# Two interleaved layers of linear attention and a squared-ReLU network: reordering the first stage and moving ten stores of the k/q weights

## The chip, the core and the metric

The kernel runs on one core of a Trainium2 chip. A core has a matrix engine (TensorE, PE in the profile, with its weight loads as PEld), a vector engine (VectorE, DVE), a scalar engine (ScalarE, ACT), a general engine (GpSimd, POOL) and a queue engine that here issues nearly all DMAs (SyncE, SP). Each engine runs its own list of instructions, and semaphores between them hold an instruction back until what it needs is there. The metric is the device time of one launch in microseconds; the median of three runs before the change is 1320.23 us.

## The reference

Two identical layers, each an attention block A and a network B, both on a residual stream `x` of 2048 rows by 640 columns:

```python
def _A_ref(x, wqkv, wo):                       # 32 heads of 20 columns
    qkv = (x @ wqkv).reshape(B, S, 3, H, Dh).transpose(2, 0, 3, 1, 4)
    q, k, v = qkv[0], qkv[1], qkv[2]
    phi = lambda t: jnp.where(t > 0, t + 1, jnp.exp(t)) + 1e-6
    pq, pk = phi(q), phi(k)
    kv = jnp.einsum("bhsd,bhse->bhde", pk, v)
    z = jnp.einsum("bhsd->bhd", pk)
    num = jnp.einsum("bhqd,bhde->bhqe", pq, kv)
    den = jnp.einsum("bhqd,bhd->bhq", pq, z)[..., None] + 1e-6
    return (num / den).transpose(0, 2, 1, 3).reshape(B, S, D) @ wo
def _B_ref(x, w1, b1, w2, b2):
    h = jnp.einsum("bsd,df->bsf", x, w1) + b1
    r = jnp.where(h > 0, h, 0)
    return jnp.einsum("bsf,fd->bsd", r * r, w2) + b2
x = A_x
x = x + _A_ref(_layernorm(x), A_wqkv, A_wo)
x = x + _B_ref(_layernorm(x), B_w1, B_b1, B_w2, B_b2)
x = x + _A_ref(_layernorm(x), A_wqkv, A_wo)
x = x + _B_ref(_layernorm(x), B_w1, B_b1, B_w2, B_b2)
```

## The kernel before

Every large product is made of three matmuls: each operand is split into a high part (a rounded copy) and a low part (what the rounding lost), and high times low, low times high and high times high are added in PSUM (`mm3`, L485). So each tile that goes into a product needs two parts: ScalarE writes the high one, VectorE then subtracts it to get the low one.

The rows are worked in 16 tiles of 128. A layer has three stages: phase A (the loop over t at L823), a transition (L960 to L1169) and the network (L1171 on). Phase A runs once through the 16 tiles, in layer 0 between about 7 and 194 us of the profile. In tile t:

- TensorE makes k and q of the tile with `part` (L574), in up to three pieces. The first goes to PSUM bank `xb[0]`, the second to `xb[1]`, the third to `xb[2]`. A tile listed in `LATE` (L43; in layer 0 tiles 9 and 11 to 15, in layer 1 tiles 8, 9, 11 and 13 to 15) makes only k in phase A, in two pieces of 320 columns; these are the q-less tiles of the title of the change, and their q is made in the transition by `late_q` (L968). The other tiles make k and q in pieces of 512, 512 and 256 columns.
- TensorE adds xᵀ·phi(k) of the tile before, t−1, to five accumulators: the strips `g_part` (L614), handed out by `gs` (L883). Every second tile it also makes two products for the last columns, `gt_part` (L620), each into a bank that a piece of k has left.
- ScalarE and VectorE turn a piece into phi: `Phi.exp` (L589, ScalarE, L591 in the profile) reads the piece in PSUM, `Phi.rest` (L594, VectorE, L598 and L599) reads it again. After the L599 of a piece its bank is free.
- For phi(k) ScalarE writes the high part (`k_post`, L783) and VectorE the low part (L793); both are the right operands of the strips, one tile later. The normalized rows are split in the same way (high L898, low L928).
- For tile t+1 the transposed rows `xT` are made ready. In layer 0 VectorE transposes in blocks (L461), ScalarE moves the blocks in 16 small copies (`move`, L803, with `turn_move`, L475), then ScalarE writes the high part (`xT_split`, L502) and VectorE the low part (L505). Eight of the 16 copies for tile t+1 are issued at the end of tile t−1 (`move(t + 2, AHEAD)`, L959), the other eight in tile t (`move(t + 1)`, L895). In layer 1 a pair of DMAs does this instead of the 16 copies.
- In tiles 1 to 13 of layer 0 the weights of the network are split on the side: `prep_step` (L809) puts up to four high parts (L301) and low parts (L313) into a tile.

The order of each engine's list is the order in which the code calls the engines; there is no scheduler, so a line that stands later in a tile waits behind all that stand before it on its engine. When a q-less tile has an even number, the list of banks is rotated at its end (L957): the first piece of tile 13 goes to the bank that the second piece of tile 12 had, and likewise for tiles 15 and 14.

The split k/q weights (`kq`, five tiles) are written to DRAM in layer 0 so that layer 1 can read them back: `keep_kq` (L195), ten DMAs of 640 KB on SP's queue, two each in tiles 11 to 15 (L832).

Of the kernel before, what the change touches and what calls it, by code (L numbers as in the profile page):

```python
# [16 lines left out]
NT = S // P  # L17
DC = D // P
# [47 lines left out]
def kernel(  # L66
# [25 lines left out]
    def bank(i, n=1):  # L92
        return PS[:, 512 * i : 512 * (i + n)]
# [17 lines left out]
    def ftile(name):  # L111
        return tmp.tile([P, D], F32, tag="f", name=name, bufs=F_BUFS)
# [38 lines left out]
    class FirstLoads:  # L151
# [19 lines left out]
        def low(self, n):  # L171
            for _ in range(min(n, len(self.halves))):
                u, raw = self.halves.pop(0)
                nc.vector.tensor_tensor(
                    out=u[:, 1], in0=raw, in1=u[:, 0].bitcast(F32), op=ALU.subtract
                )
# [18 lines left out]
    def keep_kq(c, j):  # L195
        nc.sync.dma_start(kept["kq", c][:, j], kq[c][:, j].bitcast(F32))
# [247 lines left out]
    def blocks_T(src):  # L444
        y = ftile("y")
        nc.vector.transpose(out=y, in_=src)  # L446
        return [y]
# [19 lines left out]
    def turn_move(yz, js):  # L467

        if len(yz) == 1:
            yz.append(ftile("z"))  # L470
        yv = yz[0].rearrange("p (j c q) -> p j c q", c=DC, q=B32)
        zv = yz[1].rearrange("p (c i q) -> p c i q", c=DC, q=B32)
        for j in js:
            for i in range(P // B32):
                nc.scalar.activation(  # L475
                    zv[j * B32 : (j + 1) * B32, :, i, :], yv[i * B32 : (i + 1) * B32, j], AF.Copy
                )
# [33 lines left out]
    def proj(ps, aT, w, cs=range(DC)):  # L511

        for c in cs:
            for k, l in ((1, 0), (0, 0), (0, 1)):
                for j in range(2):
                    nc.tensor.matmul(  # L516
                        ps[:, j * 512 : j * 512 + HD], aT[:, k, c, :], w[c][:, l, j * HD : (j + 1) * HD],
                        start=c == 0 and (k, l) == (1, 0), stop=c == DC - 1 and (k, l) == (0, 1),
                    )
# [28 lines left out]
    for layer in range(N_LAYERS):  # L548
# [21 lines left out]
        def xbank():  # L570
            xbanks.append(xbanks.pop(0))
            return bank(xbanks[-1])

        def part(t, a, b, ps=None):  # L574

            ps = (xbank() if ps is None else ps)[:, : b - a]
            for c in range(DC):
                mm3(
                    ps, xT[t][:, 0, c, :], xT[t][:, 1, c, :],
                    kq[c][:, 0, a:b], kq[c][:, 1, a:b], c == 0, c == DC - 1,  # L580
                )
            return ps
# [23 lines left out]
        def xtile(name, dtype=R32):  # L606
            return xp.tile([P, 2, D], dtype, tag="x", name=name, bufs=8)
# [6 lines left out]
        def g_part(t, i):  # L614

            ps = bank(GB[i])
            a, b = xh[t][:, :, i * P : (i + 1) * P], kh[t][:, :, :DM]
            mm3(ps, a[:, 0], a[:, 1], b[:, 0], b[:, 1], t == 0, t == NT - 1)

        def gt_part(p, j, ps):  # L620

            ps, rs = ps[:, :HD], slice(j * HD, (j + 1) * HD)
            for t in (2 * p, 2 * p + 1):
                a, b = kh[t][:, :, DM:], xh[t][:, :, rs]
                mm3(ps, a[:, 0], a[:, 1], b[:, 0], b[:, 1], t % 2 == 0, t % 2 == 1)
            if p == 0:
                nc.vector.tensor_copy(GT_[:, rs], ps)
            else:
                nc.vector.tensor_tensor(out=GT_[:, rs], in0=ps, in1=GT_[:, rs], op=ALU.add)
# [82 lines left out]
        def x1_at(t):  # L712
            g, i = divmod(t, TG)
            if g % 2 == 0:
                return gtile("x1")
            return x1_odd["tile"][:, i]

        def b_load_x(t):
            xr[t] = x1_at(t)
            nc.sync.dma_start(xr[t], src[t])  # L720
# [41 lines left out]
        def b_x1(t, ps):  # L762
            v = halves_sb(xr[t])
            nc.vector.tensor_tensor(out=v, in0=halves(ps), in1=v, op=ALU.add)
            ln_stats(("b", t), xr[t])
            xn[t] = ftile("xn")
            if t > 1:
                ln_apply(("b", t), by_chunk(xn[t]), by_block(xr[t]))
            else:
                ln_apply(("b", t), xn[t], xr[t])  # L770

        def f_split(t, src):
            g, j = divmod(t, TG)
            if t == 0:
                xTb[0] = tmp.tile([P, 2, DC, GT], R32, tag="T", name="xTb", bufs=2)
            sv = src[:, :D].rearrange("p (c n) -> p c n", c=DC)
            u = xTb[0][:, :, :, j * P : (j + 1) * P]
            split(u[:, 0], u[:, 1], sv)
# [24 lines left out]
        def move(t, n=JQ):  # L803

            if layer == 0 and t in yza:
                turn_move(yza[t], range(moved.get(t, 0), n))
                moved[t] = n
# [15 lines left out]
        for t in range(NT):  # L823
# [5 lines left out]
            if layer == 0:  # L829
                if t >= 14:  # L830
                    prep.store()
                if t >= NT - DC:  # L832
                    for j in range(2):
                        keep_kq(t - NT + DC, j)
            if t >= 13:
                b_load_pq(t - 13)
                load_vo(2 * t - 26)
# [45 lines left out]
            def gs(n):  # L883
                for _ in range(min(n, len(g))):
                    g_part(t - 1, g.pop(0))
# [4 lines left out]
            is_late = t in late  # L890
            f, fq = Phi(rtile()), None if is_late else Phi(ftile("rq"))
            n0 = HD if is_late else 512
            ps = ps_first if layer == 0 and t == 1 else part(t, 0, n0, bank(xb[0]))
            gs(0 if is_late or t == 1 and layer == 0 else 2)
            move(t + 1)  # L895
            f.exp(0, ps)
            xh[t] = xtile("xh")
            nc.scalar.activation(xh[t][:, 0], xt[t], AF.Copy)  # L898
            prep_step(t, 0)
# [10 lines left out]
            x_low = []  # L910
# [9 lines left out]
            f.exp(n0, ps[:, : D - n0])  # L920
            if not is_late:
                fq.exp(0, ps[:, D - n0 :])
            f.rest()
            if not is_late:
                fq.rest()
            for low in x_low:
                low()
            nc.vector.tensor_tensor(  # L928
                out=xh[t][:, 1], in0=xt[t], in1=xh[t][:, 0].bitcast(F32), op=ALU.subtract
            )  # L930
            if gt and not is_late:
                gt_part(t // 2 - 1, 0, bank(xb[0]))
            gs(1)
# [34 lines left out]
        def late_q(n=1, rest=True):  # L968

            for _ in range(n):  # L970
                if not late_parts:
                    return
                t, j = late_parts.pop(0)
                if j == 0:
                    late_phi[t] = Phi(ftile("rl"))
                late_phi[t].exp(j * HD, part(t, D + j * HD, D + (j + 1) * HD))
                late_todo.append((t, j))
                if rest:
                    late_rest()
# [3 lines left out]
        def late_rest(n=9):  # L983
            for _ in range(min(n, len(late_todo))):
                t, j = late_todo.pop(0)
                late_phi[t].rest()
                if j == 1:
                    nc.sync.dma_start(pqd[t], late_phi.pop(t).r)

        late_q(2)  # L990
        zbc = tmp.tile([P, D], F32, tag="z", name="zbc", bufs=1)
        psz = [xbank()[:, :HD] for _ in range(2)]
# [5 lines left out]
        for i in range(DC):  # L998
            g_part(NT - 1, i)
            nc.scalar.activation(G[:, i], bank(GB[i]), AF.Copy)  # L1000
        for j in range(2):
            gt_part(NT // 2 - 1, j, xbank())
        b_blocks(0)
# [14 lines left out]
        def run_side(n=1):  # L1018
            for _ in range(min(n, len(side_work))):
                side_work.pop(0)()  # L1020
# [48 lines left out]
        def m_split(m):  # L1069
            nc.vector.tensor_copy(M[m][:, 0], m_raw[m])  # L1070
            nc.vector.tensor_tensor(
                out=M[m][:, 1], in0=m_raw[m], in1=M[m][:, 0].bitcast(F32), op=ALU.subtract
            )
# [50 lines left out]

        po = {}

        for i in range(2):
            po[i] = bank(4 + 2 * i, 2)
            proj(po[i], pT[i], M, range(3))
            if i == 0:  # L1130
                m_split(4)
            run_side(2)

        def x_turned(i):

            b_x1(i, po[i])
            yzx[i] = blocks_T(xn.pop(i))
            side_work.extend(lambda k=k: turn_move(yzx[i], (k,)) for k in range(JQ))
            side_work.append(lambda: f_split(i, yzx.pop(i)[1]))

        for i in range(2):
            proj(po[i], pT.pop(i), M, range(3, DC))
            run_side(1)
            b_load_x(i + 2)
        x_turned(0)
        run_side(2)
        x_turned(1)
# [397 lines left out]
```

## Time and profile before

| | us |
|---|---|
| runs | 1320.92, 1320.23, 1320.16 |
| median | 1320.23 |
| profiled execution | 1320.5 |
| span of its core | 1318.5 |
| TensorE busy | 1310.7 |
| ScalarE busy, VectorE busy | 735.5, 865.5 |

The profile page gives the share of busy time of each engine, the chain of work that ended last and the costliest groups of instructions. The trace behind it can be asked for an engine's instructions in order of time (start, duration, line, operation, what it writes and reads, and in brackets the idle time before it with what ended that), for the waits of an engine, for the instructions that touch one tile, and for the DMAs. The granted TensorE clock is 1.00 in this execution. The time outside the span, 2.0 us, is the difference of the third and fourth lines of the table.

### The profile page before, as it was taken

Reading aid. Unit: us, or ns where it says so; the run is one execution under the profiler, and the core shown is the slowest. Engines: PE = TensorE matmul, PEld = TensorE weight load, DVE = VectorE, ACT = ScalarE, POOL = GpSimd, SP = SyncE. Lnnn points to the kernel's source line nnn. Section 1 sums busy time; section 2 is a strip of 40 time slices with the busy share of each in tenths; the row PEclk is TensorE's granted clock in tenths of the full one; section 3 lists DMA queues with packets and bytes.
Section 4 is the critical chain, followed back from the end, with each engine's and each line's share of the span. In section 5 each row is a group of like instructions: output and inputs, shape, how many; then the busy total and the mean of one; then the engine's idle time right before and its main releaser. Section 6 shows DMA issues by size and latency. Waiting matters only on the chain.

```text
span 1318.5 us, 20882 instructions
## 1 busy us (share of the span) xinstructions
PE 1310.7 (99%) x7477; PEld 1193.5 (91%) x7477; DVE 865.5 (66%) x1575; ACT 735.5 (56%) x1594; POOL 219.1 (17%) x289
## 2 busy tenths in 40 slices
PE   9999999999999999999999999999999999999998
PEld 8888889989988988998988889999899899889888
DVE  7888958767944954833856677686577559449045
ACT  5888967785475467334322233387844744854242
POOL 2333310064012002101012222001320120120000
PEclk9999999999999999999999999999999999999999
DMA  6898994499974985898954456454869659749756
GB/s 194 247 278 270 336 339 144 152 353 388 320 290 154 302 298 171 267 361 290 361 158 126 123 145 169 124 199 171 315 214 345 212 192 320 290 149 297 286 186 219
DMA packets 135036, 321.57 MB, mean 244 GB/s; under 512 B 16710, under 2 KB 61894, under 8 KB 134294
## 3 DMA queue, kind: packets, MB, share of 16 engines
q1 hardware_dynamic: 127702, 297.96, 67.1%
q0 software_dynamic: 7232, 22.29, 6.4%
q8 instruction: 59, 0.97, 0.3%
q14 instruction: 43, 0.35, 0.1%
HBM read 242.82 MB, written 65.54 MB: 234 GB/s over the span
## 4 chain that ended last, share of the span: by engine, by line
PE 91%; ACT 2%; DVE 2%; DMA 2%; SPq 1%; issue 1%; POOL 0%; ACTq 0%; DVEq 0%; POOLq 0%
PE PS L489 32%; PE PS L1204 28%; PE PS L1287 25%; PE PS L516 3%; ACT z L475 1%; PE PS L1042 1%; PE PS L1055 1%; DMA kq<-kept_kq 1%; SPq L246 1%; PE PS L849 0%; PE PS L637 0%; DMA xt<-in_A_x_dram 0%; DMA kept<-uprep 0%; DVE xT L505 0%; DVE r L599 0%
## 5 line engine op out<-in xcount | busy, mean ns | idle before, releaser
L1204 PE MATMUL PS<-xTb,u 128*128 128x512 f32 x1640 | 376.6, 389 | 0.0
L1204 PEld LDWEIGHTS PS<-xTb,u 128*128 128x128 f32 x1640 | 306.8, 188 | 62.5
L489 PE MATMUL PS<-kq,xT 128*128 128x320 f32 (+2 forms) x1575 | 285.0, 334 | 1.6 <-DVE xT L505 1.4
L489 PEld LDWEIGHTS PS<-kq,xT 128*128 128x128 f32 x1575 | 250.2, 188 | 29.8 <-DVE xT L505 2.2
L1287 PE MATMUL PS<-u,arena 128*128 128x320 f32 x1644 | 250.2, 309 | 0.0
L1287 PEld LDWEIGHTS PS<-u,arena 128*128 128x128 f32 x1644 | 243.4, 188 | 0.0
L1268 DVE TENSOR_TENSOR arena<-R,arena 128x512 fp32r<-128x512 f32 (+1 forms) x200 | 140.8, 707 | 135.3 <-ACT arena L1259 134.8
L1259 ACT ACTIVATE arena<-R 128x512 fp32r<-128x512 f32 (+1 forms) x200 | 117.9, 593 | 157.9 <-PE PS L1287 131.9
L455 ACT ACTIVATE z<-y 32x160 f32<-32x160 f32 x512 | 171.1, 334 | 49.8 <-DVE y L446 42.2
L1215 ACT ACTIVATE R<-PS,b1sb 128x512 f32<-128x512 f32 x104 | 71.5, 687 | 127.8 <-PE PS L1204 126.9
L489 PE MATMUL PS<-kh,xh 128*128 128x512 f32 x480 | 124.8, 393 | 1.0 <-DVE kh L793 0.9
L383 POOL TENSOR_SCALAR rs<-mv 128x1 f32<-128x1 f32 x64 | 34.9, 546 | 513.8 <-DVE mv L381 513.8
L489 PE MATMUL PS<-uM,pTs 128*128 128x320 f32 x720 | 109.4, 309 | 0.0
L489 PEld LDWEIGHTS PS<-uM,pTs 128*128 128x128 f32 x720 | 107.5, 188 | 1.9
L1287 PE MATMUL PS<-uw,arena 128*128 128x320 f32 x660 | 106.1, 309 | 0.0
L489 PEld LDWEIGHTS PS<-kh,xh 128*128 128x128 f32 x480 | 87.1, 188 | 16.9 <-DVE kh L793 1.8
L1287 PEld LDWEIGHTS PS<-uw,arena 128*128 128x128 f32 x660 | 99.2, 188 | 0.4 <-DVE x L1301 0.2
L1233 DVE TENSOR_TENSOR R<-R 128x512 f32<-128x512 f32 (+1 forms) x128 | 79.5, 626 | 26.0 <-ACT R L1216 26.0
L475 ACT ACTIVATE z<-y 32x160 f32<-32x160 f32 x272 | 90.9, 334 | 3.3
L591 ACT ACTIVATE r<-PS 128x512 f32<-128x512 f32 (+1 forms) x64 | 27.7, 434 | 99.4 <-PE PS L489 98.1
L1216 ACT ACTIVATE R<-R 128x512 f32<-128x512 f32 x104 | 65.8, 633 | 3.3
L598 DVE TENSOR_SCALAR r<-r 128x512 f32<-128x512 f32 (+1 forms) x64 | 21.3, 332 | 70.4 <-ACT r L591 70.2
(135 smaller groups left out, 1318.1 us busy)
## 6 DMA issues: line engine op xcount, KB each, us to landing
u<-kept SPq DMA_DIRECT2D x113, 640.0 KB, 5.6
u<-kept_w SPq DMA_DIRECT2D x104, 640.0 KB, 6.2
u<-kept SPq DMA_DIRECT2D x56, 320.0 KB, 6.1
kept<-uprep SPq DMA_DIRECT2D x49, 320.0 KB, 5.6
z<-xb SPq DMA_DIRECT2D x160, 80.0 KB, 5.3
pqt<-pq SPq DMA_DIRECT2D x32, 320.0 KB, 6.7
acc<-r POOLq DMA_DIRECT2D x28, 320.0 KB, 4.9
uw<-kept SPq DMA_DIRECT2D x14, 640.0 KB, 7.4
```

The source lines that it names most:

```text
L383: nc.gpsimd.tensor_scalar(rs, mv[:, 1:2], LN_EPS, None, op0=ALU.add)
L455: nc.scalar.activation(zv[j * B32 : (j + 1) * B32, :, i, :], yv[i * B32 : (i + 1) * B32, :, j, :], AF.Copy)
L475: nc.scalar.activation(zv[j * B32 : (j + 1) * B32, :, i, :], yv[i * B32 : (i + 1) * B32, j], AF.Copy)
L489: nc.tensor.matmul(ps, a, b, start=first and i == 0, stop=last and i == 2)
L516: nc.tensor.matmul(ps[:, j * 512 : j * 512 + HD], aT[:, k, c, :], w[c][:, l, j * HD : (j + 1) * HD], start=c == 0 and (k, l) == (1, 0), st ...
L1204: nc.tensor.matmul(ps, a[:, d, :], bb[:, d, :], start=(d, i) == order[0], stop=(d, i) == order[-1],)
L1215: nc.scalar.activation(r, v, AF.Relu, bias=b1sb[:, c : c + 1])
L1216: nc.scalar.activation(r, r, AF.Square)
L1233: nc.vector.tensor_tensor(out=quad(*out, k), in0=quad(*x, k), in1=quad(*y, k), op=op)
L1259: nc.scalar.activation(u[:, 0], v, AF.Copy)
L1268: nc.vector.tensor_tensor(out=u[:, 1], in0=v, in1=u[:, 0].bitcast(F32), op=ALU.subtract)
L1287: nc.tensor.matmul(ps, x, y, start=opens and k == 0 and p == 0 and e == 0, stop=k == PAIRS - 1 and p == b - a - 1 and e == len(seq) - 1, s ...
```

## The change

Four edits, three of them to the loop of phase A and one across phase A and the transition:

1. In layer 0 tile 2 and in layer 1 tile 1 the first two strips of the tile before stand behind the second piece instead of between the first and the second.
2. In q-less tiles the exp of the first piece stands ahead of the eight copies for the next tile (`move`), which does something in layer 0 only.
3. In q-less tiles the low part of the next tile's `xT` stands ahead of the phi of the second piece on VectorE.
4. The ten stores `keep_kq` leave tiles 11 to 15 and are issued in layer 0's transition: two before the first `late_q`, three among the last strips, and five around the first products with M.

```diff
@@ -829,9 +829,6 @@
             if layer == 0:
                 if t >= 14:
                     prep.store()
-                if t >= NT - DC:
-                    for j in range(2):
-                        keep_kq(t - NT + DC, j)
             if t >= 13:
                 b_load_pq(t - 13)
                 load_vo(2 * t - 26)
@@ -891,9 +888,12 @@
             f, fq = Phi(rtile()), None if is_late else Phi(ftile("rq"))
             n0 = HD if is_late else 512
             ps = ps_first if layer == 0 and t == 1 else part(t, 0, n0, bank(xb[0]))
-            gs(0 if is_late or t == 1 and layer == 0 else 2)
-            move(t + 1)
+            gs(0 if is_late or t + layer < 3 else 2)
+            if not is_late:
+                move(t + 1)
             f.exp(0, ps)
+            if is_late:
+                move(t + 1)
             xh[t] = xtile("xh")
             nc.scalar.activation(xh[t][:, 0], xt[t], AF.Copy)
             prep_step(t, 0)
@@ -920,6 +920,10 @@
             f.exp(n0, ps[:, : D - n0])
             if not is_late:
                 fq.exp(0, ps[:, D - n0 :])
+            if is_late:
+                for low in x_low:
+                    low()
+                x_low = []
             f.rest()
             if not is_late:
                 fq.rest()
@@ -928,6 +932,8 @@
             nc.vector.tensor_tensor(
                 out=xh[t][:, 1], in0=xt[t], in1=xh[t][:, 0].bitcast(F32), op=ALU.subtract
             )
+            if t + layer == 2:
+                gs(2)
             if gt and not is_late:
                 gt_part(t // 2 - 1, 0, bank(xb[0]))
             gs(1)
@@ -987,6 +993,13 @@
                 if j == 1:
                     nc.sync.dma_start(pqd[t], late_phi.pop(t).r)
 
+        keeps = [(c, j) for c in range(DC) for j in range(2)] if layer == 0 else []
+
+        def run_keep(n):
+            for _ in range(min(n, len(keeps))):
+                keep_kq(*keeps.pop(0))
+
+        run_keep(2)
         late_q(2)
         zbc = tmp.tile([P, D], F32, tag="z", name="zbc", bufs=1)
         psz = [xbank()[:, :HD] for _ in range(2)]
@@ -998,6 +1011,8 @@
         for i in range(DC):
             g_part(NT - 1, i)
             nc.scalar.activation(G[:, i], bank(GB[i]), AF.Copy)
+            if i % 2 == 0:
+                run_keep(1)
         for j in range(2):
             gt_part(NT // 2 - 1, j, xbank())
         b_blocks(0)
@@ -1124,6 +1139,7 @@
 
         po = {}
 
+        run_keep(2)
         for i in range(2):
             po[i] = bank(4 + 2 * i, 2)
             proj(po[i], pT[i], M, range(3))
@@ -1142,6 +1158,7 @@
             proj(po[i], pT.pop(i), M, range(3, DC))
             run_side(1)
             b_load_x(i + 2)
+            run_keep(2)
         x_turned(0)
         run_side(2)
         x_turned(1)
```

No operation is added or removed: the count of instructions and of DMAs on every engine is the same in both kernels.

## The prediction, made before the changed kernel was run

> **What bounds the kernel now.** First the page's span and busy times of each engine:
>
> ```profile
> span 1318.5 us, 20882 instructions
> ...
> PE 1310.7 (99%) x7477; PEld 1193.5 (91%) x7477; DVE 865.5 (66%) x1575; ACT 735.5 (56%) x1594; POOL 219.1 (17%) x289
> ```
>
> Then TensorE's waits (us in total, times, longest):
>
> ```profile
> PE PS L489 <- DVE xT L505: 1.4, 2, 1.2
> ...
> PE PS L489 <- DVE kh L793: 0.9, 2, 0.5
> ```
>
> TensorE sets the time: it is busy in all but 7.8 us, and the change takes no matmul away. All that it can gain is these four waits, all in phase A; all that it can lose is new ones. TensorE's list in order of time shows where the early ones stand; after it the VectorE row that guards tile 2's bank:
>
> ```profile
> 35.03 1.66 PE L489 MATMUL PS<-kh,xh 128*128 128x512 f32 x6 [0.48 <-DVE kh L793]
> ...
> 39.95 1.04 PE L489 MATMUL PS<-xh,kh 128*128 128x320 f32 x6
> ...
> 676.58 1.67 PE L489 MATMUL PS<-kh,xh 128*128 128x512 f32 x6 [0.42 <-DVE kh L793]
> ```
>
> ```profile
> 38.67 0.69 DVE L599 SCALAR_TENSOR_TENSOR r<-PS,r 128x512 f32<-128x512 f32 x1
> ```
>
> And TensorE in tiles 10 to 15 of layer 0:
>
> ```profile
> 130.86 3.56 PE L489 MATMUL PS<-kq,xT 128*128 128x512 f32 x15
> 134.26 1.52 PE L489 MATMUL PS<-kh,xh 128*128 128x512 f32 x6
> ...
> 139.02 1.04 PE L489 MATMUL PS<-xh,kh 128*128 128x320 f32 x6
> ...
> 144.65 4.56 PE L489 MATMUL PS<-kq,xT 128*128 128x320 f32 x30
> ...
> 152.47 4.56 PE L489 MATMUL PS<-kq,xT 128*128 128x320 f32 x30
> ...
> 159.82 1.04 PE L489 MATMUL PS<-xh,kh 128*128 128x320 f32 x6
> ...
> 162.23 0.38 PE L489 MATMUL PS<-kq,xT 128*128 128x320 f32 x1
> 162.87 4.51 PE L489 MATMUL PS<-kq,xT 128*128 128x320 f32 x29 [0.26 <-DVE xT L505]
> ...
> 172.13 4.52 PE L489 MATMUL PS<-kq,xT 128*128 128x320 f32 x29 [1.18 <-DVE xT L505]
> ...
> 181.71 4.56 PE L489 MATMUL PS<-kq,xT 128*128 128x320 f32 x30
> ```
>
> Tile 10 begins at 130.86, its strips at 134.26 (15 matmuls of 512 columns in 3.40 us, 0.227 each), its first gt product at 139.02; tiles 11, 12, 13 and 15 begin at 144.65, 152.47, 162.23 and 181.71; tile 14's second matmul is that at 172.13. A matmul of 320 columns takes 0.147 (1.04 us for 6 is 5 steps and a modelled end of 0.305). A wait costs about 0.16 more than its bracket, since a matmul's end is modelled past the next one's start: 0.64, 0.58, 0.42 to 0.49 and 1.34 us, 3.0 together. That is 0.23% of the time; two medians of this kernel can be told apart from about 0.2% on, 2.6 us.
>
> **Edit 1, the two early tiles.** In tile 2 the second piece takes the strips' place, and kh's low part is then long there. But the gt product behind them writes the bank of the first piece, free when the L599 at 38.67 ends, 39.36; TensorE would now be there at 39.95 − 0.64 = 39.31 and go on at about 39.40. Gain 0.55. Layer 1's tile 1 has no gt product: 0.58. Together 1.13; at least 0.5 if each meets a further short wait, at most 1.22. What is gained in tile 2 is carried on, since ScalarE keeps up with TensorE until tile 9 (it is there 0.22 early at 125.43, below).
>
> **Edits 2 and 3, the q-less tiles of layer 0.** The rows of ScalarE, then VectorE:
>
> ```profile
> 122.45 2.76 ACT L475 ACTIVATE z<-y 32x160 f32<-32x160 f32 x8
> 125.43 0.44 ACT L591 ACTIVATE r<-PS 128x320 f32<-128x320 f32 x1 [0.22 <-PE PS L489]
> 125.90 0.74 ACT L898 ACTIVATE xh<-xt 128x640 fp32r<-128x640 f32 x1
> 126.55 0.72 ACT L301 ACTIVATE uprep<-wb 128x640 fp32r<-128x640 f32 x1
> 127.17 0.72 ACT L502 ACTIVATE xT<-z 128x640 fp32r<-128x640 f32 x1
> ...
> 129.76 0.74 ACT L783 ACTIVATE kh<-r 128x640 fp32r<-128x640 f32 x1 [0.29 <-DVE r L599]
> ...
> 136.31 0.60 ACT L591 ACTIVATE r<-PS 128x512 f32<-128x512 f32 x1
> ...
> 147.09 0.44 ACT L591 ACTIVATE r<-PS 128x320 f32<-128x320 f32 x1
> ...
> 169.41 0.72 ACT L502 ACTIVATE xT<-z 128x640 fp32r<-128x640 f32 x1
> 170.04 0.42 ACT L591 ACTIVATE r<-PS 128x320 f32<-128x320 f32 x1
> ```
>
> ```profile
> 129.24 0.49 DVE L599 SCALAR_TENSOR_TENSOR r<-PS,r 128x320 f32<-128x320 f32 x1
> 129.64 0.98 DVE L505 TENSOR_TENSOR xT<-z,xT 128x640 fp32r<-128x640 f32 x1
> 130.54 0.81 DVE L928 TENSOR_TENSOR xh<-xt,xh 128x640 fp32r<-128x640 f32 x1
> ...
> 133.05 0.77 DVE L793 TENSOR_TENSOR kh<-r,kh 128x640 fp32r<-128x640 f32 x1
> ...
> 137.41 0.69 DVE L599 SCALAR_TENSOR_TENSOR r<-PS,r 128x512 f32<-128x512 f32 x1
> ...
> 159.10 0.49 DVE L599 SCALAR_TENSOR_TENSOR r<-PS,r 128x320 f32<-128x320 f32 x1
> ...
> 161.59 0.49 DVE L599 SCALAR_TENSOR_TENSOR r<-PS,r 128x320 f32<-128x320 f32 x1
> 162.00 0.81 DVE L505 TENSOR_TENSOR xT<-z,xT 128x640 fp32r<-128x640 f32 x1
> ...
> 180.12 0.49 DVE L599 SCALAR_TENSOR_TENSOR r<-PS,r 128x320 f32<-128x320 f32 x1
> ```
>
> I count on the clock of before. In tile 9 ScalarE makes its eight copies from 122.45 to 125.21 while TensorE is still at the first piece, and then waits 0.22 for it. With the exp in front it stands idle through those 2.76 us and makes the copies afterwards. Behind the exp stand the copies, xh, the next xT and the second exp, all now 2.77 late.
>
> The Trainium skill (PSUM — Partial Sum Buffer, section "Engine vs sequencer instructions") has ScalarE's queue as strictly first in, first out; this trace agrees, for xh at 125.90 needs nothing of TensorE and yet starts 25 ns after the exp. By the rule the 2.77 stand; were ScalarE able to pass a waiting exp they would be nothing, and the first rival below would come true.
>
> *Tile 10* (ScalarE 2.77 late): xT's high part ends at 127.17 + 0.72 + 2.77 = 130.66. On VectorE stands first an L313, which needs ScalarE's L301 (ended 127.27, now 130.04). A low part takes 0.81 (162.00) and gives way some 0.08 before its end (129.64 and 0.98 against 130.54), so xT's starts at 130.07 + 0.74 = 130.81 and ends at 131.63. TensorE's second matmul would need it at 130.86 + 0.23 = 131.09, as it has it now, at 130.62: with 0.05 for the semaphore 0.59 lost. The phi of tile 9's second piece comes behind, its exp 2.77 late: its L599 starts at 132.01, and the row of work from xh's low part to kh's low part starts 0.40 behind it, at 132.41 instead of 130.54. So kh's low part ends 1.87 later than 133.82; TensorE, with 14 more matmuls, is at the strips at 134.85: 0.88 lost. The first gt product takes the first piece's bank, whose L599 ends at 138.10 + 2.76 = 140.86, TensorE being there at 140.48: 0.42. Sum 1.89, against no wait today.
>
> *Tile 11*: its first piece is ready not at 147.02 (15 matmuls from 144.65 and 0.17) but 1.87 later, at 148.89. ScalarE, which today makes eight copies right ahead of 147.09, has the exp in front of them again: it is there at 147.09 − 2.78 + 2.76 = 147.07 and idles 1.82. The copies follow, and xh is 1.82 + 2.77 = 4.59 late. *Tile 12*: by the steps of tile 9 (exp 0.44, copies, xh, L301, xT) the L301 ends at 153.50, so the L313 starts at 153.53, xT's low part at 154.27, and it ends at 155.09; TensorE's second matmul needs it at 152.62 + 1.87 = 154.49: 0.65. VectorE's row of work, again begun behind phi instead of behind the low part, is about 3.5 late, as it was 1.87 at 2.77; so the first piece's L599 ends at 159.59 + 3.54 = 163.13, and the gt product that takes its bank is due at 159.82 + 1.87 + 0.65 = 162.34: 0.83.
>
> *Tile 13* shows what edit 3 does. Its first piece takes the bank of tile 12's second piece. The L599 of that ended at 162.08, before 162.23, and TensorE waited for xT's low part, right behind it. With the two swapped the L599 comes last: a low part in front of it takes VectorE for 0.74, so even without lateness it would end at up to 162.8, where TensorE starts anew today. The stall changes its releaser. And it is late: ScalarE waits for each phi before kh (the bracket at 129.76), so its lateness goes round. Of the 4.59 some 0.11 are swallowed in tile 11, where phi used to stand behind an L313 a little longer than its exp; 4.48 plus 0.16 for the low part now in front put the L599 at 162.08 + 4.64 = 166.72. TensorE is there at 162.23 + 1.87 + 0.65 + 0.83 = 165.58: 1.18 lost.
>
> *Tiles 14 and 15*: here copies and product are both ready, the order of exp and copies costs nothing, but the swap costs ScalarE 0.4 a tile (high part done at 170.13, second exp at 170.46; the low part needs 0.74). Tile 14: xT's high part ends at 170.13 + 4.62 = 174.75, its low part at 175.60, and TensorE's second matmul starts at 175.64 instead of 172.13. Tile 15 takes the bank of tile 14's second piece: its L599, 180.61 today, is 4.62 + 0.40 + 0.39 = 5.41 late, 186.02; TensorE starts at 186.06 instead of 181.71. From there ScalarE and VectorE wait for TensorE again. **The tail of phase A ends 4.35 us late**, the new waits less the two old ones.
>
> Bounds: were ScalarE late by tile 9's 2.77 alone, 1.83 less, so 2.5. If each of the eight new waits is off by 0.15 the same way, 3.1 to 5.5. The good end is −1.8, both waits gone and none new.
>
> In layer 1's q-less tiles there are no copies. The swap delays phi by at most 0.74 there, and TensorE shows no wait near it: 0, at most 0.7.
>
> **Edit 4, the stores.** It moves ten issues past SP's loads of x, M's rows and pq. The stores' landing times in phase A, the loads of w1's first units on SP, and VectorE's uses of x:
>
> ```profile
> DMA to landing us min/median/max: 6.6/7.1/13.5
> ```
>
> ```profile
> 226.94 1.38 SPq L353 DMA_DIRECT2D u<-kept_w  x3
> ```
>
> ```profile
> L764 DVE TENSOR_TENSOR x<-PS,x x4: 815/817/825, 232.8 to 248.6; 128x640 f32<-128x640 f32 x4
> ```
>
> In tiles 11 to 15 nothing on TensorE's path waits for a DMA, so taking them out gains 0. In the transition they feed no one. The narrow place is the row of x for tile 3, needed at 248.6 (the last L764): behind w1's three units, which SP issues at 0.46 each, four stores of 640 KB now stand ahead of it. Six issues more put it at about 231; at the stores' median of 7.1 us it lands near 238, at their slowest, 13.5, near 245. I take 0; the dear end is in the rivals.
>
> **Sum**: +4.35 − 0.55 − 0.58 + 0 = +3.2 us on the profiled execution's 1320.5 (2.0 of it around the span), so 1323.7. The median shown is 0.3 below that execution: 1323.4 us, 0.24% slower.
>
> **Rivals.**
> 1. *The waits go and nothing new comes*: 1320.2 − 3.0 = 1317.3, faster. For it: in tiles 12 to 14 the first piece is ready before the copies end, so exp in front costs nothing. It decides where ScalarE comes late to the exp; against it the 0.22 at 125.43, and that tile 11's piece (147.02) is ready only as the eight copies ahead of it end (147.07).
> 2. *Tile 10 swallows the lateness*: it lasts 13.79 us on TensorE (130.86 to 144.65) against 7.82 of tile 11, room for ScalarE to catch up. If its strips and its gt product have a little more room than I find, tile 11's exp comes on time, 1.83 of the lateness never arises and the tail costs 2.5: 1320.2 + 2.5 − 1.1 = 1321.6, no measurable change. Against it today's margins, 0.44 for kh's low part and 0.92 for the bank, under the 1.87 and 2.76 that come.
> 3. *The stores hold up x*: the slowest landing, 13.5, came with one or two stores in flight at a time; with four ahead, x could need half as long again, 20 us, and come at 251, 2.6 late, or twice as long, 258, 9 late: taken at 4 us it adds up to 1327.4. Against it: the median of 7.1.
>
> **How the numbers follow.** The forecast 0.60, rival 2 0.26, rival 1 0.09, rival 3 0.05. The forecast's own range is 1322.2 to 1324.6; about three quarters of it lie over the 2.6 us (0.45), a quarter below (0.15). Slower 0.45 + 0.05 + 0.01 of rival 2, 0.51; faster 0.07 of rival 1 where nearly all is gained; the rest, 0.42, the same. The range from 1318.8 to 1325.4 leaves out most of rival 1, rival 3 and little else.
>
> **What would show it.** Right: the kh waits at 35 and 676 gone, a short wait of the gt product near 39.4; in tile 9 ScalarE idle about 3 us before the exp, in tile 11 about 1.8; TensorE waiting in tile 10 for xT, kh and the L599, and tiles 13 and 15 beginning behind an L599 instead of an L505. Wrong: ScalarE's copies of tiles 9 and 11 ending where they end now; no wait in tile 10; tile 14 beginning before 172; a wait for a DMA after 230.

## The result, and the profile after

The changed kernel takes 1324.64 us (median of six runs, 1324.46 to 1326.03), the kernel before 1320.26 in six runs beside it: a ratio of 1.0034, with a 95% interval of 1.0021 to 1.0047. It is 4.4 us slower; 3.2 were forecast.

The first lines of the page of the changed kernel, then its list of TensorE's waits (us in total, times, longest):

```profile
span 1322.8 us, 20883 instructions
...
PE 1311.9 (99%) x7477; PEld 1192.7 (90%) x7477; DVE 866.9 (66%) x1575; ACT 735.3 (56%) x1594; POOL 219.8 (17%) x289
```

```profile
PE PS L489 <- DVE r L599: 2.7, 3, 1.2
...
PE PS L489 <- DVE xT L505: 1.3, 3, 0.5
PE PS L489 <- DVE kh L793: 1.2, 1, 1.2
```

The span grew by 4.3 and TensorE's busy time by 1.2. The waits for xT are still there in sum, but they are three smaller ones at other places, and waits for L599, which the list of before does not have at all, now lead it. TensorE's list in order of time, tiles 10 to 15 of layer 0 (start, duration, instruction, in brackets the wait before it):

```profile
130.19 0.40 PE L489 MATMUL PS<-kq,xT 128*128 128x512 f32 x1
131.02 3.46 PE L489 MATMUL PS<-kq,xT 128*128 128x512 f32 x14 [0.43 <-DVE xT L505]
135.66 1.66 PE L489 MATMUL PS<-kh,xh 128*128 128x512 f32 x6 [1.18 <-DVE kh L793]
...
140.82 1.15 PE L489 MATMUL PS<-xh,kh 128*128 128x320 f32 x6
...
146.57 4.63 PE L489 MATMUL PS<-kq,xT 128*128 128x320 f32 x30
...
154.47 0.30 PE L489 MATMUL PS<-kq,xT 128*128 128x320 f32 x1
155.23 4.51 PE L489 MATMUL PS<-kq,xT 128*128 128x320 f32 x29 [0.46 <-DVE xT L505]
...
163.85 1.14 PE L489 MATMUL PS<-xh,kh 128*128 128x320 f32 x6 [0.76 <-DVE r L599]
...
167.53 4.63 PE L489 MATMUL PS<-kq,xT 128*128 128x320 f32 x30 [1.16 <-DVE r L599]
...
176.38 4.52 PE L489 MATMUL PS<-kq,xT 128*128 128x320 f32 x29 [0.45 <-DVE xT L505]
...
186.92 4.64 PE L489 MATMUL PS<-kq,xT 128*128 128x320 f32 x30 [0.81 <-DVE r L599]
```

Tiles 13 and 15 (167.53 and 186.92) begin behind an L599, as the prediction said, and tile 10 has its waits for xT (131.02) and kh (135.66). This kernel enters tile 10 0.67 earlier than the kernel before (130.19 against 130.86) and tile 15 5.21 later (186.92 against 181.71): **the tail of phase A costs 5.9 us.** What stands against it is seen at four points that have the same instruction in both traces, before tile 2, behind it, at the end of layer 0's network and in layer 1 behind tile 1. The kernel before, then the changed one:

```profile
21.31 3.71 PE L489 MATMUL PS<-kq,xT 128*128 128x512 f32 x15
...
45.58 3.57 PE L489 MATMUL PS<-kq,xT 128*128 128x512 f32 x15
...
653.47 10.14 PE L1287 MATMUL PS<-u,arena 128*128 128x320 f32 x68
...
683.99 1.55 PE L489 MATMUL PS<-kh,xh 128*128 128x512 f32 x6
```

```profile
21.05 3.73 PE L489 MATMUL PS<-kq,xT 128*128 128x512 f32 x15
...
39.16 1.15 PE L489 MATMUL PS<-xh,kh 128*128 128x320 f32 x6
...
44.90 3.57 PE L489 MATMUL PS<-kq,xT 128*128 128x512 f32 x15
...
658.81 10.14 PE L1304 MATMUL PS<-u,arena 128*128 128x320 f32 x68
...
688.29 1.55 PE L489 MATMUL PS<-kh,xh 128*128 128x512 f32 x6
```

The distance of the changed kernel from the one before is −0.26, −0.68, +5.34 and +4.30. So 0.26 came ahead of tile 2, in the start that the change does not touch; tile 2 gave 0.42; the transition and the network of layer 0 added 0.13 to the 5.21; tile 1 of layer 1 gave 1.04. Together 5.88 − 0.26 − 0.42 + 0.13 − 1.04 = 4.3, the growth of the span.

### The profile page after: what moved, and what is told of

Read it like the earlier page. It is cut to its first block, busy times and chain, and to the rows that moved or that the text cites. A ratio compares the mean times of both kernels' runs of the same rounds, so it can differ in the third digit from the quotient of the medians.

```text
span 1322.8 us, 20883 instructions
## 1 busy us (share of the span) xinstructions
PE 1311.9 (99%) x7477; PEld 1192.7 (90%) x7477; DVE 866.9 (66%) x1575; ACT 735.3 (56%) x1594; POOL 219.8 (17%) x289
## 4 chain that ended last, share of the span: by engine, by line
PE 92%; DVE 3%; ACT 2%; DMA 1%; SPq 1%; issue 0%; POOL 0%; DVEq 0%
PE PS L489 33%; PE PS L1221 28%; PE PS L1304 26%; PE PS L516 3%; PE PS L1057 1%; PE PS L1070 1%; ACT z L475 1%; SPq L246 1%; DMA st<-in_B_w_dram 1%; DVE xT L505 0%; DVE uprep L313 0%; DMA kept<-uprep 0%; PE PS L846 0%; DVE bn L379 0%; DVE r L599 0%
## 5 line engine op out<-in xcount | busy, mean ns | idle before, releaser
L1318 DVE TENSOR_TENSOR x<-PS,x 128x320 f32<-128x320 f32 x112 | 53.5, 486 | 20.6 <-PE PS L1304 19.8
```

The lines of the kernel that those rows point to most:

```text
L1318: nc.vector.tensor_tensor(out=v, in0=ps, in1=v, op=ALU.add)
```

## Why ScalarE is late: tiles 9 and 11 after the change

ScalarE of the changed kernel in tile 9, then in tile 11:

```profile
124.76 0.44 ACT L591 ACTIVATE r<-PS 128x320 f32<-128x320 f32 x1 [3.01 <-PE PS L489]
125.22 2.76 ACT L475 ACTIVATE z<-y 32x160 f32<-32x160 f32 x8
...
148.97 0.44 ACT L591 ACTIVATE r<-PS 128x320 f32<-128x320 f32 x1 [2.04 <-PE PS L489]
149.43 2.76 ACT L475 ACTIVATE z<-y 32x160 f32<-32x160 f32 x8
```

The exp still starts when TensorE has the piece ready (124.76 is 125.43 less the 0.67), but ScalarE now stands idle ahead of it, 3.01 us, and makes the eight copies of 2.76 us behind it. That is the cost in one place: work that needs nothing of TensorE was put behind an instruction that waits for TensorE. VectorE of the changed kernel behind tiles 9 and 11, and GpSimd beside it:

```profile
130.15 0.82 DVE L505 TENSOR_TENSOR xT<-z,xT 128x640 fp32r<-128x640 f32 x1
130.98 0.90 DVE L598 TENSOR_SCALAR r<-r 128x320 f32<-128x320 f32 x1
131.92 0.49 DVE L599 SCALAR_TENSOR_TENSOR r<-PS,r 128x320 f32<-128x320 f32 x1
...
155.19 0.90 DVE L598 TENSOR_SCALAR r<-r 128x320 f32<-128x320 f32 x1
```

```profile
103.15 0.88 POOL L269 TENSOR_TENSOR wb<-wb,wa 128x320 f32<-128x320 f32 x1 [2.24 <-DVE uprep L313]
...
130.38 1.32 POOL L269 TENSOR_TENSOR wb<-wb,wa 128x320 f32<-128x320 f32 x1 [3.63 <-DVE uprep L313]
```

xT's low part starts at 130.15, on the clock of before 130.82, where 130.81 was worked out. But the L598 behind it takes 0.90 instead of some 0.33. It stands beside an operation of GpSimd, L269 (the last of four in the tile, a subtraction for the network's weights), that itself takes 1.32, where the same operation two tiles earlier took 0.88. This was in no term of the prediction; experiment 9 is about it.

## The experiments

Two theories were set against each other. **A**: ScalarE's lateness from edit 2 in tiles 9 and 11 goes round through VectorE and makes most of the waits. **B**: edit 3, through the banks of tiles 13 and 15, makes them. Every kernel ran in five rounds beside the kernel before; the median of that was 1320.17 for experiments 1 to 4, 1320.46 for 5 to 8 and 1320.18 for 9.

**1. Edit 1 alone**, on the kernel before:

```diff
-            gs(0 if is_late or t == 1 and layer == 0 else 2)
+            gs(0 if is_late or t + layer < 3 else 2)
...
+            if t + layer == 2:
+                gs(2)
```

> The kernel before with edit 1 alone. Both theories: phase A's tail untouched, the waits at 162.87 and 172.13 stay. In tile 2 the kh wait goes and a gt wait of about 0.1 stays (0.4 to 0.5 gained, as the trace after the change showed); in layer 1 the kh wait at 676.58 goes, 0.59 and 0.11 of the slower next matmul (0.7). If the missing wait for a kq load (0.37 and 0.11, at 665.88 before) has to do with edit 1 it goes too, otherwise it stays. So 1319.1 us (1318.6 if the load wait goes).

Measured: 1319.49 us, ratio 0.9994 (0.9985 to 1.0003), so the runs alone don't tell it from no change. In its trace the kh waits and the wait for a kq load are gone, and the two waits for xT in tiles 13 and 14 are as before. The trace gains 1.8 (0.5 in tile 2, 1.3 at layer 1's start), the medians gain 0.7; the two differ by less than the interval is wide (2.4 us), and the profiled run, 1318.69, is one of the fastest of the eleven.

**2. The change without edit 2:**

```diff
-            if not is_late:
-                move(t + 1)
-            f.exp(0, ps)
-            if is_late:
-                move(t + 1)
+            move(t + 1)
+            f.exp(0, ps)
```

> The changed kernel with edit 2 undone: copies ahead of the exp again, the rest of the change kept. Theory A (ScalarE's lateness from standing idle ahead of the exp in tiles 9 and 11 goes round and makes most of the waits): ScalarE is on time up to tile 10, the waits in tile 10 for xT, kh and the bank all go; the swap of edit 3 still puts phi 0.7 later, in tiles 9, 11, 12 and 13, so that waits for an L599 remain at tile 12's second gt product or tile 13's start (about 1.5) and tile 15's start (about 0.9). Tail +1.5 against the kernel before instead of +5.9: 1320.0 to 1321.5 us. Rival B (it is edit 3, through the banks of tiles 13 and 15, that makes the loss): the waits on L599 stay at their 2.7 and more, 1323 us or above.

Measured: 1321.59 us, ratio 1.0011 (1.0002 to 1.0019). TensorE's list from tile 10 to tile 15:

```profile
130.60 3.56 PE L489 MATMUL PS<-kq,xT 128*128 128x512 f32 x15
...
161.91 1.14 PE L489 MATMUL PS<-xh,kh 128*128 128x320 f32 x6 [1.50 <-DVE r L599]
...
164.85 4.64 PE L489 MATMUL PS<-kq,xT 128*128 128x320 f32 x30 [0.43 <-DVE r L599]
...
181.99 1.14 PE L489 MATMUL PS<-xh,kh 128*128 128x320 f32 x6 [0.85 <-DVE r L599]
...
184.36 4.56 PE L489 MATMUL PS<-kq,xT 128*128 128x320 f32 x30
```

Tile 10 has no wait that the list shows, as A has it; only its gt product comes 0.28 late, at 139.22. The swap alone makes waits for L599 of its own, and the tail costs 2.9 (−0.26 at tile 10, +2.65 at tile 15), not 1.5: the wait of 0.85 at 181.99, a gt product of tile 14 that takes the first piece's bank, was not in the expectation. So the time lies just above A's range. Of B the waits came true, 2.8 us for L599 in these three, and the time, 1323 us or above, did not.

**3. The change without edit 3:**

```diff
-            if is_late:
-                for low in x_low:
-                    low()
-                x_low = []
             f.rest()
```

> The changed kernel with edit 3 undone: xT's low part behind phi again, exp still ahead of the copies. Theory A: ScalarE is still 2.8 late from tile 9; without the swap xT's low part of tile 10 stands behind the late phi, and TensorE waits there for about 2.1 instead of 0.6 and not for kh; in tile 12 likewise 2.0; the waits for L599 become short and those for xT long, and the tail is still about +5: 1323.2 to 1324.2 us. Rival B: the waits on L599 go with the swap, 1321 us or less.

Measured: 1325.57 us, ratio 1.0036 (1.0023 to 1.0048); its five runs lie between 1323.58, the profiled one, and 1325.91. The median lies above A's 1323.2 to 1324.2, the profiled run within; the time can't be told from that of the whole change. TensorE's list:

```profile
130.14 0.39 PE L489 MATMUL PS<-kq,xT 128*128 128x512 f32 x1
132.69 3.49 PE L489 MATMUL PS<-kq,xT 128*128 128x512 f32 x14 [2.16 <-DVE xT L505]
...
156.79 4.51 PE L489 MATMUL PS<-kq,xT 128*128 128x320 f32 x29 [2.23 <-DVE xT L505]
...
186.26 4.56 PE L489 MATMUL PS<-kq,xT 128*128 128x320 f32 x30
```

The wait in tile 10 is the expected 2.1, that in tile 12 was expected at 2.0. The tail costs 5.3 (−0.72 to +4.55). So edit 2 alone costs 5.3 in the tail, edit 3 alone 2.9, both 5.9 and not 8.2: edit 3 eases the waits for xT that edit 2 makes (2.16 to 0.43 in tile 10) and pays with waits for L599. Taking edit 2 out of the change wins 3.0 in the tail, taking edit 3 out 0.6. B falls: without its edit nearly the whole loss remains.

**4. The change without edit 4:**

```diff
+                if t >= NT - DC:
+                    for j in range(2):
+                        keep_kq(t - NT + DC, j)
...
-        keeps = [(c, j) for c in range(DC) for j in range(2)] if layer == 0 else []
+        keeps = []
```

> The changed kernel with edit 4 undone: the ten stores back in tiles 11 to 15. Both theories: no wait of TensorE depends on them, 1324.6 us within 0.6. If the wait for the kq load at layer 1's start comes back the stores' place decides it, and it is 0.5 more, 1325.1.

Measured: 1325.88 us, ratio 1.0041 (1.0028 to 1.0055), which overlaps with that of the whole change; the median lies above the 1324.0 to 1325.2 expected. The waits of the tail are those of the changed kernel to within 0.02 us each. Its trace has two waits that the list of the changed kernel's lacks, one in tile 2 and one in the network:

```profile
39.85 1.15 PE L489 MATMUL PS<-xh,kh 128*128 128x320 f32 x6 [0.50 <-DVE r L599]
...
319.48 1.85 PE L1224 MATMUL PS<-xTb,u 128*128 128x512 f32 x7 [0.47 <-ACT arena L1279]
```

The first stands ahead of every one of these stores (the earliest is issued at 142.7 us in the kernel before), so it is none of edit 4's doing: ScalarE reaches the exp of tile 2's first piece 0.4 later in the tile than in the changed kernel's trace, the L599 comes as much later, and edit 1 gains nothing in tile 2 here. Where the second comes from stays open. The wait for a kq load did not come back, so the stores' place does not decide that. Whether the stores are worth up to a microsecond either way stays open; the loss is not theirs.

**5. Exp ahead of the copies only in tiles 12 to 15** (edits 1 and 4 kept, edit 3 undone):

```diff
-            if not is_late:
+            exp_first = is_late and layer == 0 and t >= 12
+            if not exp_first:
                 move(t + 1)
             f.exp(0, ps)
-            if is_late:
+            if exp_first:
                 move(t + 1)
```

> Edits 1 and 4 with the exp ahead of the copies only in tiles 12 to 15 of layer 0; edit 3 undone. Theory A (edit 2 costs only where ScalarE stands idle in front of the exp, in tiles 9 and 11): in tiles 12 to 14 the piece is long ready, so nothing is lost, the two old waits at 162.87 and 172.13 stay as they are and no other comes; 1319.5 us like edit 1 alone (1319 to 1320). Rival B (exp ahead costs in every q-less tile): 1321 us or more, with new waits from tile 13 on.

Measured: 1319.01 us, ratio 0.9989 (0.9980 to 0.9999). Its waits of the tail are the two old ones:

```profile
PE PS L489 <- DVE xT L505: 1.4, 2, 1.2
```

In tiles 12 to 15 the order of exp and copies costs and brings nothing. The loss of edit 2 lies in tiles 9 and 11 alone.

**6. Exp ahead of the copies in tile 9 alone** (the same, with `exp_first = layer == 0 and t == 9`):

> Edits 1 and 4 with the exp ahead of the copies in tile 9 alone; edit 3 undone. Theory A: ScalarE is 2.77 late behind tile 9 and never catches up before tile 15, and TensorE meets one wait of about 2.2 in tile 10 for xT's low part; in tile 11 the copies run while TensorE is late too, so no second loss; TensorE's waits for xT in tiles 13 and 14 are 0.8 and 1.2 as ScalarE sets the pace there. Tail +2.8 against before, 1321.9 us (1321.3 to 1322.6). Rival B (lateness from one tile is swallowed in tile 10): the tail is at most +1, 1320.3 us or less.

Measured: 1322.39 us, ratio 1.0013 (1.0004 to 1.0022). TensorE at tiles 10 and 15, and ScalarE's exp of tile 11:

```profile
130.39 0.40 PE L489 MATMUL PS<-kq,xT 128*128 128x512 f32 x1
132.93 3.47 PE L489 MATMUL PS<-kq,xT 128*128 128x512 f32 x14 [2.15 <-DVE xT L505]
...
184.11 2.06 PE L489 MATMUL PS<-kq,xT 128*128 128x320 f32 x13
```

```profile
149.48 0.44 ACT L591 ACTIVATE r<-PS 128x320 f32<-128x320 f32 x1
```

The tail costs 2.9 (−0.47 to +2.40), close to the 2.76 us of the eight copies. In tile 11 ScalarE goes from the copies into the exp without a wait, at 149.48 instead of 147.09, 2.9 later once the 0.47 are counted; nothing is swallowed in tile 10, and nothing is added in tile 11.

**7. A version for the same two waits.** If ScalarE's queue sets them, the cure is to fill the places where ScalarE is idle. In tiles 12 and 13 of the kernel before it waits 0.92 for phi ahead of kh's high part, while copies that need nothing stand behind:

```diff
+FILL = {11: 1, 12: 3, 13: 3}
...
+            move(t + 2, FILL.get(t, 0))
             k_post(t, f.r, [lambda: a_stats(t + 3)])
```

with `move` counting single copies instead of groups of four, and edit 1.

> A version for the same waits: the kernel before with edit 1, and in tiles 12 and 13 three, in tile 11 one, of the eight copies for the tile after next taken ahead of kh's high part, where ScalarE stands idle today for 0.92 and 0.38 until phi's L599 is done. Theory A (ScalarE's queue sets the two old waits): xT's high part of tile 13 comes 0.34 and that of tile 14 1.26 earlier; the wait at 162.87 falls from 0.49 to about 0.15, that at 172.13 from 1.33 to about 0.4; 1.3 less than edit 1 alone, 1318.2 us. Rival B (VectorE or something else sets them): no change against edit 1 alone, 1319.5 us.

Measured: 1318.28 us, ratio 0.9985 (0.9976 to 0.9994). The wait in tile 14 fell from 1.18 to 0.58 by its bracket; that in tile 13 kept its bracket of 0.26, where a wait of 0.15 in all was expected. Counted from tile 10's start, the second matmul of tile 13 comes 0.2 sooner than in the kernel before and that of tile 14 0.8, of the 1.3 expected; that the time is the expected one all the same is in part luck.

**8. The same, with xT's low part ahead of phi in tile 13 alone:**

```diff
+            if layer == 0 and t == 13:
+                for low in x_low:
+                    low()
+                x_low = []
             f.rest()
```

> The same, and in tile 13 alone xT's low part ahead of phi (edit 3 where the next tile's bank isn't the one that this phi frees). Theory A: the rest of the wait in tile 14 goes too, no wait for L599 comes; 0.4 less than without, 1317.8 us. Rival B: the phi behind it is late for the next tile, and the gain is given back, 1318.2 us or more.

Measured: **1317.81 us, ratio 0.9980 (0.9971 to 0.9989)**, faster than the kernel before and than the changed one. ScalarE in tile 12, where three copies fill the former wait, then the one wait of phase A that TensorE's list of waits still shows beyond the start (this kernel's lines are one higher: L476 is the copies, L784 kh's high part, L506 xT's low part):

```profile
160.47 1.01 ACT L476 ACTIVATE z<-y 32x160 f32<-32x160 f32 x3
161.51 0.74 ACT L784 ACTIVATE kh<-r 128x640 fp32r<-128x640 f32 x1
```

```profile
PE PS L490 <- DVE xT L506: 0.2, 1, 0.2
```

Against experiment 7 the step is 0.5 and the intervals overlap, but the wait at tile 14's start is gone from the list. Edit 3 in a tile whose phi frees no bank for the next tile's first piece, and with ScalarE's idle time in tile 12 filled, saves 0.8 at tile 14's start and costs 0.2 later in tile 14.

**9. The changed kernel without GpSimd's last L269 in tiles 9 and 11** (the expectation calls it an addition, by the code it subtracts; the kernel leaves that part of the network's weights out):

```diff
-                    self.then.pop(key[0])()
+                    last = self.then.pop(key[0])
+                    if key[0] not in (3, 4):
+                        last()
```

> The changed kernel without GpSimd's third addition (L269, wb) in tiles 9 and 11; it leaves that part of the prepared network weights out, so its output differs, while all other instructions stay. Theory (the larger part of what the tail cost beyond the forecast is VectorE's L598 of 0.90 instead of 0.33 us while that addition runs beside it): L598 in tiles 9 and 11 takes 0.33; TensorE's wait for kh in tile 10 falls from 1.18 to about 0.6, the short one in tile 12 goes, and ScalarE is up to 1.1 less late in tiles 12 to 15, so 1323.6 us (1323.2 to 1324.2). Rival (L598 is long for another reason, as the low part written just before it): it stays at 0.90, and 1324.6 us.

Measured: 1323.56 us, ratio 1.0027 (1.0016 to 1.0037), 1.1 less than the whole change. The two intervals overlap, but the traces agree: from tile 10's start to tile 15's it is 55.60 us here (130.07 to 185.67) and 56.73 in the changed kernel. VectorE at xT's low part of tile 10 and the phi behind it, then TensorE at tile 10's strips (this kernel's lines are two higher: L600 is the former L598):

```profile
130.04 0.82 DVE L507 TENSOR_TENSOR xT<-z,xT 128x640 fp32r<-128x640 f32 x1
130.87 0.33 DVE L600 TENSOR_SCALAR r<-r 128x320 f32<-128x320 f32 x1
```

```profile
134.97 1.66 PE L491 MATMUL PS<-kh,xh 128*128 128x512 f32 x6 [0.59 <-DVE kh L795]
```

The instruction takes 0.33 where it took 0.90, with xT's low part still right ahead of it, and the wait for kh is 0.59 instead of 1.18. The L269 of GpSimd was the cause.

## Why the prediction was right, and where its size was off

The direction, the mechanism and the places were right; 1324.64 lies in the range given, just above the forecast's own. That the sum came so near is in part luck: the tail cost 1.5 us more than forecast, while layer 1's tile 1 gave 0.46 more than forecast and the start was 0.26 shorter, which no term held.

- **Edit 1.** Tile 2: forecast −0.55 with a short wait of the gt product left near 39.4; measured −0.42, with that wait at 39.16 for L599. The gain is not steady: from tile 2's first matmul to tile 3's the changed kernel's trace gains 0.45, those of the nine experiments, which all hold edit 1, from 0.04 (experiment 4) to 0.50 (experiment 8). Layer 1: forecast −0.58, measured −1.04. The kh wait is gone, and of the wait for a kq load, which the matmuls of before show with 0.21 and its weight loads with 0.64, the weight loads still show 0.33 (at 670.92). Experiments 1 to 9 show none of it. The load took 9.6 us from issue to landing in the trace of before, 9.2 in the changed kernel's and 8.3 to 9.0 in the others; what sets that time wasn't tried, and as all the others hold edit 1, its part in it stays open.
- **Edit 2.** The idle times of 3 and 1.8 us ahead of the exp in tiles 9 and 11 were 3.01 and 2.04. Edit 2 in tile 9 alone was given 2.5 as a bound and cost 2.9 in experiment 6, there without edit 3. That it costs nothing in tiles 12 to 14 is shown by experiment 5.
- **The eight waits** in tiles 10 to 15 all came, each for the instruction named, and a ninth with them: kh's low part in tile 12, an idle time of 0.12. On the clock of tile 10's start the points of the sum compare so (the measured ones are the rows above plus 0.67):

| | before | forecast | measured |
|---|---|---|---|
| tile 11 begins | 144.65 | 146.54 | 147.24 |
| tile 12 begins | 152.47 | 154.34 | 155.14 |
| tile 13 begins | 162.23 | 166.76 | 168.20 |
| tile 14, second matmul | 172.13 | 175.64 | 177.05 |
| tile 15 begins | 181.71 | 186.06 | 187.59 |

- **The mis-sized term** is the tail: +4.35 forecast, 5.88 measured. The step that failed is "its L599 starts at 132.01": it started at 131.92 + 0.67 = 132.59, since the L598 ahead of it took 0.90 instead of 0.33. The sum goes off by 0.70 in tile 10, and by as much again between tiles 12 and 13, behind the second L598 of 0.90; from there the distance stays. Experiment 9 took both away and gained 1.1 of the 1.5; what the other 0.4 come from no run shows by itself. Before the change this L598 (at 128.87) hardly met an L269. The trace of before had the price all the same: the L598 of tile 9's first piece, at 127.09, took 0.53 beside the L269 that runs from 126.55 to 127.43. VectorE's rows of tile 9, then GpSimd's:

```profile
127.09 0.53 DVE L598 TENSOR_SCALAR r<-r 128x320 f32<-128x320 f32 x1
...
128.87 0.33 DVE L598 TENSOR_SCALAR r<-r 128x320 f32<-128x320 f32 x1
```

```profile
129.02 0.93 POOL L269 TENSOR_TENSOR wb<-wb,wa 128x320 f32<-128x320 f32 x1 [1.59 <-DVE uprep L313]
```

  The last L269 is released by the L313 ahead of phi. Phi followed that L313 at once; in the changed kernel it comes 0.7 behind it, after xT's low part and the late exp, and so falls into the L269.
- **Edit 3** was costed with edit 2 and never alone. Alone it costs 2.9 in the tail (experiment 2), more than either the text or the expectation of that experiment gave it.
- **Edit 4**, taken at nothing: TensorE's matmuls show no wait for a DMA behind 230 us in the changed kernel, only its weight loads the 0.33 named above, less than before. Experiment 4's median is 1.2 us above the changed kernel's, with overlapping intervals, so a worth of that size is neither shown nor excluded.
- **The rivals.** That all waits go (1317.3) fell with the idle time ahead of the exp; a version without that idle time does come to it (1317.8, experiment 8). Tile 10 swallows no lateness (experiment 6). The stores held up no row of x that VectorE's list would show: it has no wait for a DMA between 195 and 262 us.

## What to carry to other kernels

In an engine's list the work that waits for nothing belongs ahead of an instruction that waits for another engine, and the order is judged tile by tile: the same swap cost 2.9 us where the piece came late and nothing where it had long been ready. On an engine that sets the pace, look for the places where it is idle and move work into them; seven copies put into three such gaps took 0.8 us off the tail (experiment 7), where the swap added 2.9 in one tile alone. When the lateness of one engine is carried forward by hand, ask also what the late instruction will stand beside when it runs.

## What the runs showed of the hardware

- VectorE's L598 (a tensor by a scalar, 128x320 in f32) takes 0.33 us alone and 0.90 beside GpSimd's L269, which takes 0.88 alone and 1.32 there. Both lose: the L269 begins at 130.38, while xT's low part runs to 130.97, and takes 0.44 more than alone; the L598 begins at 130.98, takes 0.57 more and ends 0.18 behind the L269's end at 131.70. The Trainium skill (SBUF — State Buffer, section "SBUF: two separate sides") says that some of VectorE's instructions, among them those with two inputs in SBUF, and GpSimd's take a shared pair of ports as an exclusive lock, by which the loser stands still until the other's instruction is done. The trace agrees to some 0.15 us: by the overlaps of these rows the two would have lost 0.59 and 0.72, and they lost 0.44 and 0.57.
- A wait of TensorE costs about 0.27 us more than its bracket, not the 0.16 of the prediction, because the matmuls behind it start slowly too: six matmuls of 320 columns take 1.15 behind the wait at 140.82 and took 1.04 without one, at 139.02 before. With 0.27 each, the nine waits of the tail less the two old ones come to 5.9 us, what the tail costs.
